# Wide weights for state times r, routing of four chunks at a time, other transfer splits and a re-planned order in a linear-attention and mixture-of-experts kernel

## The chip, the cores and the metric

One core of one Trainium2 chip runs the whole program in one launch. The metric is the device time in microseconds. The kernel before was run three times: 624.01 us median, 620.74 to 625.52.

## The reference

The first half is a recurrence over 768 time steps for 4 batches x 8 heads, head size 40, in float32. The second half routes each of the 3072 resulting rows of 320 values to one of 8 experts.

```python
for t in range(S):                                   # S = 768, state is [B,H,40,40]
    y[:, :, t] = einsum('bhd,bhde->bhe', r_t, state)
    Sa = einsum('bhde,bhe->bhd', state, a_t)
    state = state * w_t[:, :, None, :] - Sa (x) b_t + v_t (x) k_t
x = y as [3072, 320]
skip = x @ w_skip > 0 ; logits = x @ w_gate ; e = argmax(logits)
h = relu(x @ w1[e]) ; out = x + gate * (h @ w2[e])   # rows with skip > 0, else out = x
```

## The kernel before

**Tiling of the recurrence.** The 768 steps are cut into 24 chunks of 32 steps (`c`), two chunks to a block of 64 (`h`), four chunks to a phase (`ph`). The 32 batch-head pairs are two groups of 16 (`x` is 0 or 1, the upper and the lower partitions). Partitions 0 to 39 hold one half of the batches, 64 to 103 the other. Within a chunk the recurrence is solved in closed form: products of w by scans (`scan_z`, `scan_w`), small products of a, b and k (`m1`), the inverse of a triangular 32x32 system (`tinv`, on DVE), and then per chunk and group the chain that carries the state.

**The chain of one chunk.** `rs` multiplies the state by r (even chunks alone, for 64 steps), `ux` applies the left factors, `uq` the triangular inverse, followed by four ACT copies into the tile R1t and a POOL multiplication that masks R1t; `sst` makes the next state (ACT and DVE copies of it go to R1t and, in odd chunks, to the tile SS); `yy` makes the chunk's 128 x 320 output rows, which DVE scales into the tile XS and which SP writes to `out`. The two groups run half a chunk apart. `m2` multiplies v by r for the next chunk.

**SS and rs.** SS is [128, 2, 8, 40]: for each half of the batches a block whose other half of the partitions is zero. `rs` (line 534) runs 16 matmuls per group and even chunk, each with 40-column weights and 64 moving columns, alternating between output partitions 0 to 39 and 64 to 103.

**Routing.** After every second chunk `RP` (line 697) starts `route` (line 894) on two chunks: three transposes per chunk, `score` (line 869, 12 matmuls in four strips of 32 output partitions), `pick` (line 875, small DVE operations on 128 x 16 values), 8 matmuls that count rows per expert, more DVE operations, and one indirect POOL transfer per chunk that scatters the rows to the DRAM tensor `xg`. The last two chunks are routed one by one, in the gap between the two halves of the program.

**Transfers.** SP issues nearly all of them from one in-order queue: w, k and b, a (`load_w`, `load_kb`, `load_a`), v (`load_v`, line 366), zeros (`l1z`, line 405), the mask copies of `m1` (4 per call), the padding of `xg` (`pad`, line 860), expert weights (`load`, line 944), chunk outputs. The repeated copies of v and r (`load_rv`, line 357, `load_rr`, line 362) are issued by POOL except in the first chunk.

**What sets the order.** The recorder `Rec` (from line 62) collects all operations up to chunk 22, estimates each one's time with hand-fitted constants (line 68, `cost` at line 100, `pipe` at line 122 for transfers), and `plan` (line 184) lists them greedily by due time (`keys`, line 258). `flush` (line 262) then emits them in that order, so all planned operations carry line 272 in the profile; operations recorded outside the plan carry line 134. `plan` also has a model of the arrival of PE's instructions in blocks of 256 (constants BLK and SLOW).

**Experts.** From about 480 us on, each expert's weights are split into a high and a low part and two products per layer part are run on PE; rows are scattered to `out`.

Of the kernel before, what the change touches and what calls it, by code (L numbers as in the profile page):

```python
# [62 lines left out]
class Rec:  # L63
# [3 lines left out]
    HOP={'PA':0.066,'VA':0.034,'AV':0.033,'PV':0.11,'AP':0.053,'VP':0.055,'GP':0.054,'AG':0.08,'VG':0.13,'PG':0.17}  # L67
    EX=dict(V=0.08,P=0.07,A=0.0,G=0.0,S=0.0); PW=1.25; BLK=3.6; SLOW=0.8; BW=2.7e5; DSC=0.012; AHEAD=2.5
    def hop(s,e,f): return (0.114 if e=='V' else 0.0) if e==f else s.EX[e]+s.HOP.get(e+f,0.04)
# [30 lines left out]
    def cost(s,e,op,w,r,a):  # L100
        sz=lambda x: int(np.prod([d[1] for d in list(x.ap)[1:]])) if len(list(x.ap))>1 else 1
        n=max(sz(x) for x in (w[:1]+r[:1]))
        if 'dma' in op: return (1.06,2.6) if 'ind' in op else (0.63 if e=='S' else 0.55,2.2)
        ps=any('PSUM' in str(x.space).upper() for x in r)
        if e=='P':
            o=sz(w[0]); m=w[0].ap[0][1]
            if op=='transpose': return max(0.145,0.04+0.001*o),0
            if m<16: return 0.05+0.0016*o,0
            if m==16: return 0.022,0
            if m==32: return 0.034 if o<16 else 0.0098+0.00041*o,0  # L110
            if m<=48: return 0.0213+0.00072*o,0
            if m<=64: return max(0.072,0.028+0.00075*o),0
            return max(0.11,0.0021*o),0
        if e=='A': return 0.15+0.00085*n+(0.06+0.07*(n>99) if op=='activation' else 0.12 if abs(w[0].ap[-1][0])>8 and n>99 else 0.0),0
        if e=='G': return (0.08+n*0.0008 if op=='memset' else 0.18 if op=='tensor_copy' else 0.2+0.00195*n),0
        if op=='tensor_tensor_scan': return 0.02+0.00217*n,0
        if op=='transpose': return 0.08+0.00115*n*(1 if n<1000 else 1.6),0
        if op=='memset': return 0.04+0.0003*n,0
        if op=='reciprocal': return 0.17,0
        if op=='tensor_tensor': return (0.1 if ps and 'PSUM' not in str(w[0].space).upper() and n>199 else 0.06)+0.00105*n*(1 if ps or n<99 else 1.75),0  # L120
        return 0.12+0.00105*n,0
    def pipe(s,w,r):

        n=int(np.prod([d[1] for d in w.ap])); run=n
        for x in (w,r):
# [4 lines left out]
            run=min(run,q)  # L130
        p=w if 'DRAM' not in str(w.space).upper() else r
        return 4*n/min(6e5,5e3*max(16,p.ap[0][1]))+n/run*s.DSC/16
    def call(s,e,op,fn,a,k):
# [50 lines left out]
    def plan(s,keep=None):  # L184
# [33 lines left out]
        while done<N:  # L218
# [20 lines left out]
            if e=='P':  # L239
                pos+=t.k  # L240
                while pos>=256*(blk+1):
                    x=max(fin[i],ent+s.BLK); fin[i]=x; ent=x; blk+=1
            if t.L and e in 'VG': port[e]=fin[i]
# [3 lines left out]
            elif e=='G' and t.f==2: gi=-1.0  # L247
            if t.x: dq=max(dq,fin[i]+1.0)+t.x; lat=max(lat+t.x,dq+1.2-fin[i])
            for j in t.n:
# [6 lines left out]
        s.st,s.fin,s.bank_of,s.en,s.span=st,fin,bank,en,max(fin)  # L256
    LET=0.7; FAR=1.0; ALT=1.0; FILL=None
    def keys(s):
# [46 lines left out]
def attn(ctx,tc,i,m,out,X):  # L305
# [5 lines left out]
    pp=m.pp  # L311
# [26 lines left out]
    RW=(104,72)  # L338
    SS=[cp.tile([128,2,8,40],F32,name=f"SS{x}") for x in range(2)]
    eo=(0,64); ao=(64,0); uo=(96,32)  # L340
# [15 lines left out]
    rvt={}  # L356
    def load_rv(c,E=G):
        if c>=NC: return
        t=VV[0] if c%2==0 else RR[1] if c==1 else VV[1]
        rvt[c]=t.rearrange("p (u t) -> p u t",u=16); cutl(E,rvt[c],i['vv'][c],c<4,128)  # L360
    rrt={}
    def load_rr(h,E=G):

        if h>=NH: return
        rrt[h]=RR[h%2].rearrange("p (u t) -> p u t",u=16); cutl(E,rrt[h],i['rr'][h],h<2,128)
    def load_v(c,x):
        if c>=NC: return
        SP.dma_start(R1[x][c%NR1][ao[x]:ao[x]+32,:,0:40],i['vt'][c,x])
    def scan_z(h,dst=None,E=None,rv=rv):
# [35 lines left out]
    def l1z(h,x):  # L405
        if h>=NH: return
        SP.dma_start(L1[x][h%NL][ao[x]:ao[x]+32].rearrange('p u c t -> p (u c t)'),i['zer'][0:32,0:1024])
    def l1a(h,x,E=None):
# [125 lines left out]
    def rs(c,x):  # L534
# [5 lines left out]
        for hh in range(4):  # L540
            for b in (0,2,1,3):
                s=slice(64*(b//2),64*(b//2)+40); v=(b%2)*4+hh
                TE.matmul(RS[s,v,:],SS[x][:,b//2,v,:],rr[:,b%2,2*hh+x,:],start=True,stop=True)
        for bh in range(2):
# [26 lines left out]
    def sst(c,x):  # L571
# [22 lines left out]
        for bh in range(2):  # L594
            s=slice(64*bh,64*bh+40)
            A.copy(SS[x][s,bh],S2[s])
    Yt={}; XS={}
    def yy(c,x):
# [8 lines left out]
        if x==1:  # L607
            if cc==0: XS[c//2]=m.xp.tile([128,2,XW],F32,tag="XS",name="XS")
            xs=XS[c//2][:,cc,0:320]
            V.tensor_tensor(xs.rearrange("p (h e) -> p h e",h=8),Y,H[c//2]['WT',cc].rearrange("p h x e -> p (h x) e"),ALU.mult)  # L610
# [8 lines left out]
    if 1:  # L619

        with tc.manual_schedule(engines={ET.Pool}):
            rec.on=True
            z,zl=(SS[x].rearrange("p a b c -> p (a b c)") for x in range(2))
            fl=lambda t: t.rearrange("p u c t -> p (u c t)")
# [5 lines left out]
            V.memset(fk(KBa[0][96:128]),0.0); G.memset(fk(KBa[1][96:128]),0.0)  # L630
            V.memset(rv,0.0); V.memset(z[:,0:512],0.0); V.memset(zl,0.0)
            G.memset(WR[:,8192:10240],0.0)
# [6 lines left out]
            for x in range(2): load_v(0,x)  # L639
            load_rv(0,SP); load_rr(0,SP); load_kb(2)  # L640
            scan_z(0,None,V); scan_d(0); scan_w(0,V); load_w(2)
# [8 lines left out]
            for x in range(2): l1a(1,x,V)  # L650
            load_a(2,L1t[:,3072:4096].rearrange("p (u t) -> p u t",u=16)); load_rv(1,SP)
            for b in range(4): kbt(0,b)
# [6 lines left out]
            for x in range(2):  # L659
                for c in range(2): SP.dma_start(L2[x][0][64*x:64*x+64,c],i['idl'][x,64*x:64*x+64])  # L660
            load_kb(3); load_w(3,alt[:,0:1041]); load_a(3,a1)
# [7 lines left out]
            load_w(4); load_kb(4)  # L669
            G.memset(z[:,512:640],0.0); G.memset(L1t[:,2048:3072],0.0)  # L670
            m2(1,0); Tb(4); m2(1,1); Tb(3)
# [18 lines left out]
            for x in range(2):  # L690
                for c in range(2): SP.dma_start(L2[x][1][64*x:64*x+64,c],i['idl'][x,64*x:64*x+64])
        tg=iter(()); tn=[0]
# [4 lines left out]
        def RP(p):  # L697
            nonlocal rg
            if c%2==0 and c>0 and p==ROUTE[0]: rg=m.route(XS[c//2-1],2,c-2)
            if p in (RLAST[c-22] if c>21 else ROUTE[1+c%2]):  # L700
                if c>1 and p in RB[c%2]: burst(1,m.tri,m.mc[:,0:RN])
                next(rg,None)
        def last22():
            xl=XS[NC//2-1]
            def onehot(q): V.tensor_scalar(m.P[q],m.io,m.sl[:,0:1],None,ALU.is_equal)
            return xl,m.route(xl[:,0:1],1,NC-2,lambda: onehot(0)),onehot
        for c in range(NC):
# [93 lines left out]
            T()  # L801
            load_rv(c+2,G if c else SP)
            if c%2 or c==0: load_rr((c+3)//2,G if c else SP)
            if c<2: m.pad(2*c); m.pad(2*c+1)
# [42 lines left out]
class Moe:  # L847
# [12 lines left out]
    def pad(s,k):  # L860
        s.nc.sync.dma_start(s.xg.rearrange("(q p) d -> p q d",p=128)[:,4*k:4*k+4],s.i['xpad'].unsqueeze(1).broadcast_to([128,4,XW]))
    def xpose(s,X):
# [6 lines left out]
    def score(s,xT,sc):  # L869
        nc=s.nc  # L870
        lg=s.ps.tile([128,9],F32,tag="pp",name="lg")
        for k,(a,b) in enumerate(KT):
            for q in range(4): nc.tensor.matmul(lg[32*q:32*q+32],xT[:b-a,k,32*q:32*q+32],s.wg[:b-a,k,:],start=k==0,stop=k==2)
        nc.scalar.copy(sc,lg)
    def pick(s,pr,n,gate):
# [18 lines left out]
    def route(s,XS,n,c0,last=None):  # L894
# [246 lines left out]
```

## Time and profile before

| | us or share |
|---|---|
| median of 3 runs | 624.01 |
| the profiled execution's own time | 625.9 |
| its span, first to last instruction | 624.0 |
| PE busy | 470.0 (75%), 12424 matmuls |
| DVE busy | 472.7 (76%), 1269 |
| ACT busy | 390.0 (62%), 982 |
| POOL busy | 315.5 (51%), 285 |
| mean granted TensorE clock | 0.923 of full speed |
| DMA packets | 64360, 80.59 MB, 129 GB/s over the span |

PE is TensorE's matmul side, PEld its weight loads, DVE VectorE, ACT ScalarE, POOL GpSimd, SP SyncE. A busy PE is a modelled figure: matmuls overlap. Idle time is put down to the last releaser seen; "issue" means that the engine waited for nothing that the profile shows. Each float32 matmul of the program stands in the trace as two matmuls and two weight loads.

### The profile page before, as it was taken

To read this page: it belongs to the slowest core of one execution; us is meant where nothing else is said; L and a number is where in the kernel's file an instruction comes from. 1 tells how busy PE (TensorE), PEld (TensorE's weight loads), DVE (VectorE), ACT (ScalarE), POOL (GpSimd) and SP (SyncE) were. 2 spreads that over 40 slices of the span, in tenths; PEclk is the share of its full clock that TensorE was granted. 3 is DMA by queue.
4 is the path that set the end of the run, shared out by engine and by line. 5 is a ranking of instruction groups with operands and counts; after the bars stand their busy time and mean duration, and the time that the engine had idled before them with its cause. 6 is when DMAs were issued, how large, how long until landed. Compare 5 with 4: busy or idle time off the path is not lost. (4 is left out here: it accounts for less than half of the span.)

```text
span 624.0 us, 28751 instructions
## 1 busy us (share of the span) xinstructions
PE 470.0 (75%) x12424; PEld 407.5 (65%) x12424; DVE 472.7 (76%) x1269; ACT 390.0 (62%) x982; POOL 315.5 (51%) x285
## 2 busy tenths in 40 slices
PE   0154327877787887887887789878977999999992
PEld 0143216666666666776776677667765799999992
DVE  6525894789997987998989879865783558898860
ACT  7073216878695877887696769577865455555510
POOL 4133626437491868477583853234223266666751
PEclk9997757899897998998798989989988999999997
DMA  8997232433452453425351534453663477775100
GB/s 190 251 270 226 78 99 65 130 81 92 93 137 75 108 143 100 133 67 147 87 153 40 144 98 109 101 153 95 167 168 93 123 220 232 240 225 156 43 18 18
DMA packets 64360, 80.59 MB, mean 129 GB/s; under 512 B 33698, under 2 KB 52719, under 8 KB 63124
## 3 DMA queue, kind: packets, MB, share of 16 engines
q1 hardware_dynamic: 58323, 64.55, 38.6%
q0 software_dynamic: 5904, 14.15, 8.2%
q8 instruction: 99, 1.62, 1.2%
q14 instruction: 34, 0.27, 0.1%
HBM read 67.80 MB, written 13.15 MB: 130 GB/s over the span
## 5 line engine op out<-in xcount | busy, mean ns | idle before, releaser
L272 ACT COPY R1t<-pc 32x288 f32<-32x288 f32 (+4 forms) x254 | 98.8, 389 | 38.1 <-PE pc L272 32.4
L272 POOL TENSOR_TENSOR R1t<-R1t,mc 64x512 f32<-64x512 f32 x43 | 55.5, 1292 | 70.9 <-ACT R1t L272 64.7
L272 DVE TENSOR_TENSOR px<-px,M 128x168 f32<-128x168 f32 (+10 forms) x240 | 61.2, 265 | 2.3
L134 POOL TENSOR_TENSOR WL<-WR,WH 128x1280 fp32r<-128x1280 f32 (+1 forms) x21 | 57.8, 2794 | 8.6 <-ACT WH L134 8.6
L272 POOL TENSOR_TENSOR WR<-WR,M 104x1024 f32<-104x1024 f32 x19 | 41.6, 2207 | 35.5 <-DVE M L272 22.9
L272 DVE TENSOR_TENSOR M<-M,px 128x168 f32<-128x168 f32 (+10 forms) x240 | 54.4, 255 | 2.0 <-DVE px L272 0.2
L272 DVE TENSOR_TENSOR_SCAN M<-M 104x1041 f32<-104x1041 f32 (+1 forms) x20 | 47.0, 2348 | 0.2
L272 ACT COPY R1t<-pq 32x256 f32<-32x256 f32 (+4 forms) x101 | 36.2, 358 | 8.4 <-PE pq L272 5.3
L134 ACT CAST WH<-WR 128x1024 fp32r<-128x1024 f32 (+1 forms) x35 | 39.6, 1132 | 0.0
L272 POOL DMA_INDIRECT xg<-XS,ix x20 | 24.1, 1206 | 29.9 <-DMA xg<-XS,ix 11.7
L134 POOL DMA_INDIRECT out<-ro,ti x16 | 15.8, 989 | 44.3 <-DVE ro L134 10.7
L272 PE MATMUL pc<-UX,TB 32*32 32x104 f32 (+1 forms) x1024 | 30.2, 245 | 9.0 <-issue 7.9
L134 ACT ACTIVATE hH<-pc 128x512 fp32r<-128x512 f32 x21 | 12.6, 599 | 37.8 <-PE pc L134 37.8
L134 DVE CAST ti<-xe 128x2 int32<-128x2 f32 x8 | 35.0, 4376 | 0.2
L272 PE MATMUL py<-L2t,R1t 128*32 128x40 f32 x1344 | 23.4, 208 | 12.1 <-issue 9.4
L134 PE MATMUL pc<-xH,WH 128*128 128x256 f32 x126 | 32.5, 283 | 0.0
L272 DVE TENSOR_TENSOR R1t<-pc,D 40x512 f32<-40x512 f32 (+1 forms) x44 | 26.6, 605 | 6.3 <-PE pc L272 4.2
L134 DVE TENSOR_TENSOR WL<-WR,WH 128x1024 fp32r<-128x1024 f32 (+1 forms) x19 | 23.8, 1253 | 9.9 <-ACT WH L134 9.4
L272 ACT COPY R1t<-ps 40x288 f32<-40x288 f32 (+4 forms) x72 | 27.5, 383 | 5.4 <-PE ps L272 4.2
L272 PE MATMUL ps<-R1t,L2t 128*40 128x72 f32 (+1 forms) x672 | 28.6, 233 | 2.8 <-ACT R1t L272 1.6
L272 PEld LDWEIGHTS pc<-UX,TB 32*32 32x32 f32 x1024 | 21.5, 107 | 14.0 <-issue 10.1
L272 PEld LDWEIGHTS py<-L2t,R1t 128*32 128x32 f32 x1344 | 17.7, 114 | 16.3 <-issue 11.7
(353 smaller groups left out, 1537.0 us busy)
## 6 DMA issues: line engine op xcount, KB each, us to landing
WR<-w SPq DMA_DIRECT2D x16, 640.0 KB
WR<-w SPq DMA_DIRECT2D x16, 512.0 KB
WR<-kb SPq DMA_DIRECT2D x16, 320.0 KB
WR<-w SPq DMA_DIRECT2D x16, 256.0 KB
R1t<-vt SPq DMA_DIRECT2D x48, 80.0 KB
out<-XS SPq DMA_DIRECT2D x24, 160.0 KB
rrt<-rr POOLq DMA_DIRECT2D x20, 160.0 KB, 5.4
vvt<-vv POOLq DMA_DIRECT2D x20, 160.0 KB, 6.1
```

What stands on the lines that cost most here:

```text
L134: if not s.on: return fn(*a,**k)
L272: for fn,a,k,own in s.tasks[i].calls: (fn if s.en[i]==s.tasks[i].e else s.nc.vector.tensor_copy)(*[at(x,own) for x in a],**{n:at(x,own) fo ...
```

## The change

The state tile becomes [128, 8, 104]: both halves of the batches stand on the diagonal of one 104-column block, and `rs` runs 8 matmuls with 104-column weights where it ran 16 with 40. Routing takes four chunks at a time (chunks 0 to 19), then two, then one and one; score and counting use the full 128 output partitions in place of four strips. `load_rv` and `load_rr` move from POOL's queue to SP's. The DRAM side of several transfers (v, zeros, the identity blocks, padding, the weights of experts 0 and 1) gets an outer dimension of 8. The planner's constants and its transfer model change, and with them the order of everything up to chunk 22. The scratch that software-issued transfers get is set to 4096 bytes a partition.

```diff
-    EX=dict(V=0.08,P=0.07,A=0.0,G=0.0,S=0.0); PW=1.25; BLK=3.6; SLOW=0.8; BW=2.7e5; DSC=0.012; AHEAD=2.5
+    EX=dict(V=0.08,P=0.07,A=0.0,G=0.0,S=0.0); PW=1.25; BLK=3.4; SLOW=0.0; BW=2.0e5; AHEAD=2.5; LAND=1.7
...
-        if 'dma' in op: return (1.06,2.6) if 'ind' in op else (0.63 if e=='S' else 0.55,2.2)
+        if 'dma' in op: return (1.06,2.6) if 'ind' in op else (0.63 if e=='S' else 0.55,0.0)
...
-        p=w if 'DRAM' not in str(w.space).upper() else r
-        return 4*n/min(6e5,5e3*max(16,p.ap[0][1]))+n/run*s.DSC/16
+        return max(4*n/s.BW,n/run*0.002)
...
-                    x=max(fin[i],ent+s.BLK); fin[i]=x; ent=x; blk+=1
+                    x=max(fin[i],ent+s.BLK+s.SLOW*min(8.0,max(0.0,dq-ent))); fin[i]=x; ent=x; blk+=1
...
-            if t.x: dq=max(dq,fin[i]+1.0)+t.x; lat=max(lat+t.x,dq+1.2-fin[i])
+            if t.x:
+                a=fin[i]+(0.5 if e=='S' else 1.5); b=max(dq,a); dq=b+t.x
+                if t.x<0.3: b=a+0.4*(b-a)
+                lat=b+t.x+s.LAND-fin[i]
...
-    LET=0.7; FAR=1.0; ALT=1.0; FILL=None
+    LET=0.7; FAR=1.25; ALT=1.0; FILL=None
...
-    SS=[cp.tile([128,2,8,40],F32,name=f"SS{x}") for x in range(2)]
+    SS=[cp.tile([128,8,104],F32,name=f"SS{x}") for x in range(2)]
...
-    def load_rv(c,E=G):
+    def load_rv(c,E=SP):
...
-    def load_rr(h,E=G):
+    def load_rr(h,E=SP):
...
-        SP.dma_start(R1[x][c%NR1][ao[x]:ao[x]+32,:,0:40],i['vt'][c,x])
+        SP.dma_start(R1[x][c%NR1][ao[x]:ao[x]+32,:,0:40],i['vt'][c,x].rearrange('(a b) u d -> a b u d',a=8))
...
         for hh in range(4):
-            for b in (0,2,1,3):
-                s=slice(64*(b//2),64*(b//2)+40); v=(b%2)*4+hh
-                TE.matmul(RS[s,v,:],SS[x][:,b//2,v,:],rr[:,b%2,2*hh+x,:],start=True,stop=True)
+            for b in range(2): TE.matmul(RS[0:104,b*4+hh,:],SS[x][:,b*4+hh,:],rr[:,b,2*hh+x,:],start=True,stop=True)
...
-            A.copy(SS[x][s,bh],S2[s])
+            A.copy(SS[x][s,:,64*bh:64*bh+40],S2[s])
...
-            if cc==0: XS[c//2]=m.xp.tile([128,2,XW],F32,tag="XS",name="XS")
-            xs=XS[c//2][:,cc,0:320]
+            if c%4==0: XS[c//4]=m.xp.tile([128,4,XW],F32,tag="XS",name="XS")
+            xs=XS[c//4][:,c%4,0:320]
...
-            if c%2==0 and c>0 and p==ROUTE[0]: rg=m.route(XS[c//2-1],2,c-2)
+            if c%4==0 and c>0 and p==ROUTE[0]: rg=m.route(XS[c//4-1],4,c-4)
+            if c==22 and p==ROUTE[0]: rg=m.route(XS[5][:,0:2],2,20)
...
                 next(rg,None)
+                if c<22: next(rg,None)
...
-            load_rv(c+2,G if c else SP)
-            if c%2 or c==0: load_rr((c+3)//2,G if c else SP)
+            load_rv(c+2)
+            if c%2 or c==0: load_rr((c+3)//2)
...
-        s.nc.sync.dma_start(s.xg.rearrange("(q p) d -> p q d",p=128)[:,4*k:4*k+4],s.i['xpad'].unsqueeze(1).broadcast_to([128,4,XW]))
+        s.nc.sync.dma_start(s.xg.rearrange("(q p) d -> p q d",p=128)[:,4*k:4*k+4],s.i['xpad'].rearrange('(a b) d -> a b d',a=8).unsqueeze(2).broadcast_to([8,16,4,XW]))
...
-            for q in range(4): nc.tensor.matmul(lg[32*q:32*q+32],xT[:b-a,k,32*q:32*q+32],s.wg[:b-a,k,:],start=k==0,stop=k==2)
+            nc.tensor.matmul(lg,xT[:b-a,k,:],s.wg[:b-a,k,:],start=k==0,stop=k==2)
...
-        rk=s.ps.tile([128,2*n,8],F32,tag="pp",name="rk")
-        for q in range(4): nc.tensor.matmul(rk[32*q:32*q+32,0:n,:],s.tri[:,32*q:32*q+32],oh,start=True,stop=True)
-        for q in range(4): nc.tensor.matmul(rk[32*q:32*q+32,n:2*n,:],s.one[:,0:32],oh,start=True,stop=True)
+        rk=s.ps.tile([128,n+1,8],F32,tag="pp",name="rk")
+        nc.tensor.matmul(rk,s.tri,s.oh[:,0:n+1],start=True,stop=False)
+        for j in range(n): nc.tensor.matmul(rk[:,j+1:n+1],s.one,oh[:,j].unsqueeze(1).broadcast_to([128,n-j,8]),start=False,stop=j==n-1)
         ps=wk.tile([128,n,8],F32,tag="pos",name="pos")
-        for j in range(n):
-            nb=wk.tile([128,8],F32,tag="base",name="base",bufs=3)
-            V.tensor_tensor(ps[:,j],rk[:,j],s.base,ALU.add)
-            V.tensor_tensor(nb,rk[:,n+j],s.base,ALU.add); s.base=nb
+        V.tensor_tensor(ps,rk[:,0:n],s.base.unsqueeze(1).broadcast_to([128,n,8]),ALU.add)
+        nb=wk.tile([128,8],F32,tag="base",name="base",bufs=3)
+        V.tensor_tensor(nb,rk[:,n],s.base,ALU.add); s.base=nb
...
+        n=8 if e<2 else 16
+        for k in range(2): SP.dma_start(r[:,1024*k:1024*k+1024],s.i['w1'][e,128*k:128*k+128].rearrange('(a b) f -> a b f',a=n))
...
-    nc = bacc.Bacc("TRN2", target_bir_lowering=False, num_devices=1)
+    nc = bacc.Bacc("TRN2", target_bir_lowering=False, num_devices=1, dynamic_dma_scratch_size=4096)
```

## Rows read from the trace of the kernel before

**Rows 1.** Stretches: length, then busy us (count) of PE, PEld, DVE, ACT, POOL; clock, DMA.
```profile
0.00:60.00 60.00, 15.57 (x364) 13.35 (x364) 29.81 (x34) 29.96 (x70) 19.20 (x18) 0.95 0.90 240
60.00:100.00 40.00, 14.60 (x630) 12.31 (x631) 32.85 (x62) 9.81 (x29) 18.30 (x27) 0.59 0.29 82
100.00:480.00 380.00, 308.74 (x10402) 255.13 (x10399) 312.93 (x1036) 288.34 (x797) 202.38 (x202) 0.94 0.44 113
480.00:624.00 144.00, 131.07 (x1040) 126.71 (x1033) 97.14 (x138) 61.87 (x87) 75.59 (x39) 0.97 0.47 139
...
400.00:480.00 80.00, 65.19 (x2139) 53.02 (x2137) 52.77 (x159) 58.13 (x163) 24.99 (x25) 0.94 0.49 134
140.00:400.00 260.00, 210.85 (x6995) 174.95 (x6996) 230.16 (x783) 197.50 (x546) 159.82 (x161) 0.93 0.43 109
```

**Rows 2.** Waits from 100 to 480 us: waiter, releaser, us in total, times, longest.
```profile
PEld pc L272 <- issue: 17.9, 32, 3.9
PEld py L272 <- issue: 11.7, 15, 3.3
PEld pq L272 <- issue: 6.7, 16, 1.6
PEld ps L272 <- issue: 5.9, 20, 1.3
...
POOL R1t L272 <- ACT R1t L272: 64.7, 17, 11.4
```

**Rows 3.** Page, DMA queues: packets, MB, share of 16 engines.
```profile
q8 instruction: 99, 1.62, 1.2%
```

**Rows 4.** Timeline from 184 to 200 us: start, us, work, idle before it and releaser.
```profile
196.54 1.19 PE L272 MATMUL pc<-UX,TB 32*32 32x104 f32 x31 [3.78 <-issue]
197.66 1.08 PE L272 MATMUL pc<-WR,L1t 128*32 128x64 f32 x32
197.78 2.02 ACT L272 COPY R1t<-pc 32x416 f32<-32x416 f32 x4 [5.14 <-PE pc L272]
...
199.88 1.28 POOL L272 TENSOR_TENSOR R1t<-R1t,mc 64x512 f32<-64x512 f32 x1 [11.37 <-ACT R1t L272]
```

**Rows 5.** Whole span, instructions on SS, then on xT, then on oh alone.
```profile
0.00:624.00 624.00, 26.60 (x704) 22.91 (x704) 2.53 (x5) 17.25 (x41) 0.20 (x1) 0.92 0.48 129
...
0.00:624.00 624.00, 12.27 (x576) 9.69 (x576) 3.90 (x12) 10.04 (x36) 0.92 0.48 129
...
0.00:624.00 624.00, 4.43 (x208) 3.31 (x208) 10.88 (x39) 0.92 0.48 129
```

**Rows 6.** PE timeline of single groups: start, us, work.
```profile
226.79 0.22 PE L272 MATMUL pq<-rrt,SCR 128*64 128x32 f32 x1
...
125.64 0.66 PE L272 MATMUL pc<-rrt,SCR 128*64 128x32 f32 x16
...
115.93 0.69 PE L272 MATMUL pc<-rrt,vvt 128*64 128x64 f32 x16
...
117.84 1.09 PE L272 MATMUL pq<-rrt,SS 128*40 128x64 f32 x32 [0.28 <-ACT R1t L272]
...
139.03 0.49 PE L272 MATMUL pq<-wg,xT 128*32 128x9 f32 x24
...
263.58 0.32 PE L272 MATMUL ps<-oh,mc 128*32 128x16 f32 x16
```

**Rows 7.** DVE timeline of a routing of two chunks: start, us, work.
```profile
159.60 0.18 DVE L272 TENSOR_TENSOR eq<-sc,mx 128x16 f32<-128x16 f32 x1
159.70 0.17 DVE L272 TENSOR_TENSOR sb<-sc,mx 128x16 f32<-128x16 f32 x1
```

**Rows 8.** POOL groups from 100 to 480 us: busy, mean ns, idle before and releasers.
```profile
L272 POOL DMA_INDIRECT xg<-XS,ix x20 | 24.1, 1206 | 29.9 <-DMA xg<-XS,ix 11.7 <-DVE px L272 7.8 <-PE pc L134 4.9
...
L272 POOL DMA_DIRECT2D vvt<-vv x20 | 11.0, 557 | 7.2 <-PE pc L272 6.2 <-PE pq L272 1.0
L272 POOL DMA_DIRECT2D SCR<-vv x20 | 10.8, 548 | 14.3 <-PE pc L272 9.1 <-PE pq L272 4.6 <-PE ps L272 0.6
L272 POOL DMA_DIRECT2D rrt<-rr x18 | 9.2, 518 | 0.0
```

**Rows 9.** Timeline of SP's queue from 60 to 300 us.
```profile
102.62 0.60 SPq L272 DMA_DIRECT2D R1t<-vt  x1
```

**Rows 10.** DMA issues up to 60 us: work, count, KB each.
```profile
xg<-xpad SPq DMA_DIRECT2D x3, 644.0 KB
```

More of the change, by code (lines that the diff above doesn't have):

```diff
@@ L406, in l1z @@
         if h>=NH: return
-        SP.dma_start(L1[x][h%NL][ao[x]:ao[x]+32].rearrange('p u c t -> p (u c t)'),i['zer'][0:32,0:1024])
+        SP.dma_start(L1[x][h%NL][ao[x]:ao[x]+32].rearrange('p u c t -> p (u c t)'),i['zer'][0:32,0:1024].rearrange('(a b) f -> a b f',a=8))
     def l1a(h,x,E=None):
@@ L622, in attn @@
             rec.on=True
-            z,zl=(SS[x].rearrange("p a b c -> p (a b c)") for x in range(2))
+            z,zl=(SS[x].rearrange("p a b -> p (a b)") for x in range(2))
             fl=lambda t: t.rearrange("p u c t -> p (u c t)")
@@ L630, in attn @@
             V.memset(fk(KBa[0][96:128]),0.0); G.memset(fk(KBa[1][96:128]),0.0)
-            V.memset(rv,0.0); V.memset(z[:,0:512],0.0); V.memset(zl,0.0)
+            V.memset(rv,0.0); V.memset(z,0.0); V.memset(zl,0.0)
             G.memset(WR[:,8192:10240],0.0)
@@ L639, in attn @@
             for x in range(2): load_v(0,x)
-            load_rv(0,SP); load_rr(0,SP); load_kb(2)
+            load_rv(0); load_rr(0); load_kb(2)
             scan_z(0,None,V); scan_d(0); scan_w(0,V); load_w(2)
@@ L650, in attn @@
             for x in range(2): l1a(1,x,V)
-            load_a(2,L1t[:,3072:4096].rearrange("p (u t) -> p u t",u=16)); load_rv(1,SP)
+            load_a(2,L1t[:,3072:4096].rearrange("p (u t) -> p u t",u=16)); load_rv(1)
             for b in range(4): kbt(0,b)
@@ L659, in attn @@
             for x in range(2):
-                for c in range(2): SP.dma_start(L2[x][0][64*x:64*x+64,c],i['idl'][x,64*x:64*x+64])
+                for c in range(2): SP.dma_start(L2[x][0][64*x:64*x+64,c],i['idl'][x,64*x:64*x+64].rearrange('(a b) u d -> a b u d',a=8))
             load_kb(3); load_w(3,alt[:,0:1041]); load_a(3,a1)
@@ L669, in attn @@
             load_w(4); load_kb(4)
-            G.memset(z[:,512:640],0.0); G.memset(L1t[:,2048:3072],0.0)
+            G.memset(L1t[:,2048:3072],0.0)
             m2(1,0); Tb(4); m2(1,1); Tb(3)
@@ L690, in attn @@
             for x in range(2):
-                for c in range(2): SP.dma_start(L2[x][1][64*x:64*x+64,c],i['idl'][x,64*x:64*x+64])
+                for c in range(2): SP.dma_start(L2[x][1][64*x:64*x+64,c],i['idl'][x,64*x:64*x+64].rearrange('(a b) u d -> a b u d',a=8))
         tg=iter(()); tn=[0]
@@ L702, in RP @@
                 next(rg,None)
+                if c<22: next(rg,None)
         def last22():
-            xl=XS[NC//2-1]
+            xl=XS[5][:,2:4]
             def onehot(q): V.tensor_scalar(m.P[q],m.io,m.sl[:,0:1],None,ALU.is_equal)
@@ L886, in pick @@
         m2=wk.tile([128,n],F32,tag="m2",name="m2"); V.reduce_max(m2,eq,axis=AX.X)
-        oh=wk.tile([128,n,8],F32,tag="oh",name="oh"); V.tensor_tensor(oh,eq,b3(m2),ALU.is_equal)
+        oh=wk.tile([128,5,8],F32,tag="oh",name="oh"); V.memset(oh[:,n],0.0); s.oh=oh; oh=oh[:,0:n]; V.tensor_tensor(oh,eq,b3(m2),ALU.is_equal)
         V.scalar_tensor_tensor(oh,pr[:,:,8:9].broadcast_to([128,n,8]),0.0,oh,ALU.is_gt,ALU.mult)
@@ L946, in load @@
         SP=s.nc.sync; r=s.raw[e%2]
-        for k in range(2): SP.dma_start(r[:,1024*k:1024*k+1024],s.i['w1'][e,128*k:128*k+128])
-        for k in range(2): SP.dma_start(r[64*k:64*k+64,2048:3072],s.i['w1'][e,256:320])
-        for k in range(2): SP.dma_start(r[:,3072+1280*k:4352+1280*k].rearrange("p (k d) -> p k d",k=4),s.i['w2'][e,512*k:512*k+512].rearrange("(k p) d -> p k d",p=128))
+        n=8 if e<2 else 16
+        for k in range(2): SP.dma_start(r[:,1024*k:1024*k+1024],s.i['w1'][e,128*k:128*k+128].rearrange('(a b) f -> a b f',a=n))
+        for k in range(2): SP.dma_start(r[64*k:64*k+64,2048:3072],s.i['w1'][e,256:320].rearrange('(a b) f -> a b f',a=n))
+        for k in range(2): SP.dma_start(r[:,3072+1280*k:4352+1280*k].rearrange("p (k d) -> p k d",k=4),s.i['w2'][e,512*k:512*k+512].rearrange("(k a b) d -> a b k d",k=4,a=n))
     def base_last(s):
```

## The prediction

> **What bounds the kernel now.** First the busy times by stretch [rows 1]. Four stages show. Up to 60 us the transfers are the full resource (share 0.90, 240 GB/s). From 60 to 100 us it is DVE (32.9 of 40). From 100 to 480 us no engine is full: PE 308.7, DVE 312.9, ACT 288.3 and POOL 202.4 of 380. From 480 us PE is busy 131 of 144, and the change touches next to nothing there. So the change is decided between 100 and 480 us. Which engine sets that stage's pace can be read from its two parts: from 140 to 400 us DVE is busy 89% of the time, after 400 us only 66%, yet PE stays at 81% in both and runs 26.9 and 26.7 matmuls per us. Emptying DVE by a quarter did not speed PE up. I therefore count PE's time nearly in full, DVE's and POOL's at about a quarter.
>
> Then the waits of this stage [rows 2]. What stops PE's weight loads most often is "issue": 17.9 + 11.7 + 6.7 + 5.9 = 42.2 us in 83 stalls. The page has 99 instruction packets on one queue [rows 3], and PE runs 2 x 12424 = 24848 weight loads and matmuls, about 251 a packet. Between 100 and 480 us that makes 2 x 10402 / 251 = 83 packets: as many as stalls. I read them as PE waiting for its next packet, 0.51 us each. The timeline shows what a long one does [rows 4]: PE stops inside `uq` for 3.78 us, ACT then stands 5.14 us and POOL 11.37 us.
>
> **The change, part by part.** The sum is made against the profiled execution's 625.9 us (span 624.0); the median, 624.01, is 1.9 lower.
>
> *Fewer PE instructions.* SS is read by 704 recorded matmuls: 22 groups (11 even chunks, two x) of 32, two records per matmul of the code [rows 5]. They become 352. The 576 score records (24 per chunk) become 144, the 208 counting records 64 (five routings of four chunks at 10, one of two at 6, two of one at 4). That is 928 matmuls and as many weight loads, 1856 of 24848 instructions, 7.4 packets. At 0.51 us a stall they give 3.8 us. Two more effects lower the stalls that stay. PE work that grows (next part) by 20 us over 76 packets can fill up to 0.26 us of each stall; I take half, 10 us. And a packet's transfer shares its engine with data for 0.44 of the time [rows 1]; if data moves to fewer engines and the packets' engine is not among them, up to 0.44 of the remaining 28 us goes. No view shows engine numbers, so I take half of that, 6 us. Together -20; ends 0 (nothing on the path) and -42 (all stalls).
>
> *Wider PE weights.* The trace has no 104-wide weights with few moving columns. Nearest are the groups of v times r: 16 passes in two halves side by side, 8 steps with 64-wide weights; they take 0.66 us with 32 moving columns and 0.69 with 64 [rows 6]. The moving columns hardly count, so the weights set the step: with the last pass at 0.22 us, (0.66 - 0.22)/7 = 0.063 us, 1 ns a column. Then 104 columns cost 0.10 us and 128 cost 0.126. `rs` now takes 1.09 us for 32 passes, two side by side; after, 16 passes one after the other, 15 x 0.10 + 0.22 = 1.72: +0.63, times 22 = +14. Score: 5 x 0.126 + 0.22 = 0.85 against 0.49, times 24 = +8.6. Counting: 1.35 against two times 0.32 in five routings, 0.85 against 0.32 in one, 0.60 against 0.32 in two, +4.7. Upper end +27. Lower end -1: if moving columns set the step as in today's `rs` ((1.09 - 0.22)/15 = 0.058 us), `rs` stays at 1.09 us and score and counting keep their strips' pace. I take +20: the 64-wide row is the nearest, less a quarter, because a group's first weights can load while the group before runs.
>
> The Trainium skill speaks against the change here: "TensorE: Matmul & The Clock Gate", section "LDWEIGHTS (loading the stationary operand)", gives the load as columns divided by 1.2 in ns, whatever the rows, so 87 ns for 104 columns and 107 for 128; the 64-wide row agrees (53 ns against 63). By it the three would add 9.6 + 6.4 + 3.6 = +20 in place of +27, less a quarter +15 in place of +20.
>
> *DVE.* A routing of two chunks runs 18 small operations, one of four 17; ten of the first kind become five of the second, 95 fewer. They start 0.10 us apart and last 0.17 to 0.18 [rows 7], so 9.5 to 17 us of DVE. At a quarter: -3; ends 0 and -17.
>
> *POOL.* The 58 plain transfers issued there from 100 to 480 us cost 11.0 + 10.8 + 9.2 = 31.0 us of busy time and held POOL 7.2 + 14.3 = 21.5 us for buffers that PE was still reading [rows 8]. Queued behind them are the R1t masks, for which `yy` and `sst` wait. But in 17 of some 46 masks POOL was ready and waited for ACT, 64.7 us in all [rows 2]; only the others can have been late. -8; ends 0 and -21.5.
>
> *SP.* It gets these 58 issues at 0.60 us [rows 9], +35 us, and their waits for buffers, with `m1`'s mask copies and v queued behind. SP is otherwise idle or waiting, so this costs only where a needed copy is next: +2; ends 0 and +10 (half of the 21.5).
>
> *Scatters.* Of 20 scatters half follow another directly; now three in four do, 5 more, each behind the one before for 11.7/6 = 1.95 us [rows 8]: 10 us of POOL, with masks behind. +2; ends 0 and +10.
>
> *Start.* Up to 60 us 240 GB/s x 60 = 14.4 MB move [rows 1], of which padding is 1.9 MB [rows 10] and identity and v by the code some 1.0 MB. If those 2.9 MB go to 8 engines, the busiest get (14.4 - 2.9)/16 + 2.9/8 = 1.08 MB in place of 0.90, 20% more, up to +12 us. But padding is needed only by the first scatter and most of it was issued late, and DVE sets the next 40 us. 0; ends -5 and +12. State zeroing, the larger XS and the smaller scratch cost nothing here: the first lies under the loads of the start, the others are space; without that cover the zeroing is under 1 us.
>
> *New order.* No row prices it. One stall as in [rows 4] either way is some 10 us; the plan now has a landing time of its own, so -3; ends -10 and +10.
>
> *Expert stage.* PE sets it; the weights of experts 0 and 1 arrive on fewer engines but are asked for well before 480 us: 0; ends 0 and +6.
>
> Sum: -20 + 20 - 3 - 8 + 2 + 2 + 0 - 3 = -10: 615.9 profiled, **614** as a median.
>
> **The rivals.** (1) The instruction supply sets the whole pace: 7.4 packets at 380/83 = 4.6 us each, -34, the wider weights hidden under it and the rest -10: 580, up to 600 if half so. For it: a stall for each packet. Against: PE is busy 81%. (2) No change: wider weights eat what the supply gives, and the chain PE, ACT, POOL of `uq` keeps its pace because neither POOL nor DVE decided it: 620 to 626. For it: the 64.7 us that POOL waits for ACT. (3) Slower: the array becomes the bound. The 104- and 128-wide weights cost their full +27, and only the 3.8 us come back, with -3 - 8 + 4 from the others: +16, 640. For it: the flat 0.66 and 0.69; it decides if an `rs` group takes 1.7 us and the issue waits stay over 35 us. (4) Slower through transfers: fewer engines for the loads, +12 at the start and +8 behind SP's head: 634. For it: the 0.90 share up to 60 us. The split could also do nothing, if the number of engines doesn't follow that dimension; then the 6 us of the supply go and so does this rival: 620.
>
> The Trainium skill has a rule on this: "DMA: Bandwidth & Descriptors", section "Why a DMA increments its semaphore by 16 and not by 1", says that the engines used are the largest number up to 16 that divides both sides' slowest dimensions, and on SP's queue the lowest-numbered ones. By that rule the split does what it says; no row here shows it.
>
> **How the numbers follow.** Two runs of one kernel differ by under 1%, so 1% is what can be told. Forecast: 0.50 (0.44 of it under 617.8), own range 605 to 620. Rival 1: 0.12, faster. Rival 2, with the split that does nothing: 0.20, within 1%. Rivals 3 and 4: 0.09 each, slower. Faster 0.56, within 1% 0.26, slower 0.18. The range from 596 to 633 leaves out most of rival 1 and of rival 3 and the far side of 4, some 0.2.
>
> **What would show it.** In the trace after: 11496 matmuls and some 92 instruction packets; `rs` groups of 16 at about 1.7 us (right) or 1.1 (wrong); PEld's issue waits from 42 to about 22 us; POOL without plain transfers after the start; DVE less by 10 to 17 us. The prediction is wrong if the issue waits hardly fall, if the first chunk's output comes later than before, or if the stage's length follows DVE or POOL.

## The result and the profile after

The changed kernel takes **607.22 us** (median of four runs, 602.21 to 612.9) beside 624.21 for the kernel before: a ratio of 0.971, 95% interval 0.963 to 0.979. In two later groups of runs it gave 0.970 (0.961 to 0.978) and 0.973 (0.968 to 0.978). Forecast were 614, a range of 596 to 633 and a narrower one of 605 to 620. Some executions take over 1.5% longer than the fastest of their kernel, many of them at a lower granted clock; the ratios, and the medians in the first column of the table of experiments, leave them out.

The profiled execution took 606.73 us, with a span of 604.7. By stretch (columns as in [rows 1]):

```profile
0.00:60.00 60.00, 19.66 (x552) 16.76 (x552) 56.76 (x77) 36.02 (x87) 33.94 (x34) 0.87 0.75 206
60.00:100.00 40.00, 24.42 (x1005) 21.13 (x1005) 25.94 (x69) 20.22 (x56) 15.81 (x15) 0.69 0.60 165
100.00:462.00 362.00, 314.00 (x8923) 267.67 (x8924) 284.72 (x884) 272.62 (x755) 166.31 (x137) 0.94 0.42 114
462.00:604.00 142.00, 134.73 (x1024) 129.22 (x1023) 99.63 (x141) 61.85 (x87) 75.38 (x39) 0.97 0.47 141
```

The change was expected to be decided in the third stretch. The largest difference stands in the first: DVE is busy 56.8 of 60 us where it was busy 29.8 [rows 1]. Where the time went is read best from the one instruction that writes each chunk's output. These are the VectorE groups of it, the first two lines of before and the last two of after: count, shortest, median and longest in ns, then the start of the first and the last in us. The first line of each pair holds chunks 0 to 20, the second 21 to 23:

```profile
L272 DVE TENSOR_TENSOR XS<-py,WT x21: 475/491/494, 111.9 to 444.3; 128x320 f32<-128x320 f32 x21
L134 DVE TENSOR_TENSOR XS<-py,WT x3: 491/492/493, 461.9 to 480.2; 128x320 f32<-128x320 f32 x3
```

```profile
L274 DVE TENSOR_TENSOR XS<-py,WT x21: 473/485/493, 96.2 to 415.9; 128x320 f32<-128x320 f32 x21
L133 DVE TENSOR_TENSOR XS<-py,WT x3: 492/492/492, 443.4 to 462.8; 128x320 f32<-128x320 f32 x3
```

| stretch | before | after | difference |
|---|---|---|---|
| start, to the first output | 111.9 | 96.2 | -15.7 |
| first to 21st output | 332.4 | 319.7 | -12.7 |
| 21st to 22nd output | 17.6 | 27.5 | +9.9 |
| 22nd to 24th output | 18.3 | 19.4 | +1.1 |
| last output to the end | 143.8 | 141.9 | -1.9 |

So the 19.3 us of the two spans are three things: a shorter start, a faster middle, and 10 us given back in one place.

**The start.** Waits of DVE up to 60 us, before (waiter, releaser, us in total, times, longest):

```profile
DVE M L272 <- ACT M L272: 17.3, 3, 11.0
DVE XS L272 <- DMA mc<-mc: 10.7, 1, 10.7
```

After, none of them is over 0.8 us. In the timeline of DVE (start, us, work, idle before it and releaser; two lines of before, then two of after), the transposes that before began at 46.49 us, behind an 11 us wait, begin at 29, and the copy from `mc` that before stopped DVE for 10.7 us until 22.4 stands at 40:

```profile
22.40 0.25 DVE L272 COPY XS<-mc 128x2 f32<-128x2 f32 x2 [10.68 <-DMA mc<-mc]
...
46.49 0.32 DVE L272 STREAM_TRANSPOSE M<-pc 128x128 f32<-128x128 f32 x1 [10.99 <-ACT M L272]
```

```profile
28.99 0.29 DVE L274 STREAM_TRANSPOSE M<-pq 128x128 f32<-128x128 f32 x1
...
40.16 2.07 DVE L274 COPY XS<-mc 128x4 f32<-128x4 f32 x1
```

The 11 us wait for ScalarE goes back to transfers as well. In PE's queue before (timeline: start, us, work, idle before it and releaser) the products of v and r stand ahead of the work that DVE is waiting for, and PE waits for their loads:

```profile
30.26 1.12 PE L272 MATMUL pc<-rrt,vvt 128*64 128x64 f32 x16 [6.83 <-DMA rrt<-rr]
...
39.66 1.07 PE L272 MATMUL pq<-rrt,rrt 128*64 128x32 f32 x16 [6.54 <-DMA rrt<-vv]
```

An early instruction that waited for a late transfer held everything behind it on its engine. After, these products begin at 35.93 and 46.19 us, behind the work that they held up. On SP's queue the first loads of v and r for them are issued at 21.50 and 21.90 us (before at 7.94 and 12.44), the next ones (`R1t<-vt`) from 37.24 (14.79) and the identity blocks from 40.88 (27.48), while the third load of w comes at 12.38 in place of 21.86. The transfers spread out, 0.75 and 0.60 of the DMA engines' time in the first two stretches where [rows 1] has 0.90 and 0.29.

**The 10 us given back.** POOL from 412 us, then PE's weight loads (timeline: start, us, work, idle before it and releaser):

```profile
412.65 1.01 POOL L274 DMA_INDIRECT xg<-XS,ix  x1 [0.16 <-issue]
...
418.47 0.98 POOL L274 DMA_INDIRECT xg<-XS,ix  x1 [4.81 <-DMA xg<-XS,ix]
...
426.67 0.97 POOL L274 DMA_INDIRECT xg<-XS,ix  x1 [7.22 <-DMA xg<-XS,ix]
429.43 1.26 POOL L274 TENSOR_TENSOR R1t<-R1t,mc 64x512 f32<-64x512 f32 x1 [1.79 <-DMA xg<-XS,ix]
430.74 0.60 PEld L133 LDWEIGHTS py<-L2t,R1t 128*32 128x32 f32 x32 [8.60 <-POOL R1t L274]
```

The scatters of chunks 16 to 19 stand in a row (the first of them is at 407.41, with one mask behind it). The third and the fourth wait until the one before has landed. The next R1t mask is queued behind them, and `yy` on PE waits 8.6 us for the mask. The wait also costs clock: the granted clock is 1.00 from 400 to 420 us, 0.81 from 420 to 430, where PE is busy 1.5 us, and 0.50, its lower level of 1.2 GHz, from 430 to 435.

**PE.** Three groups in the timeline after, which answer to [rows 6]: score, `rs`, counting for four chunks:

```profile
399.27 0.93 PE L274 MATMUL pc<-wg,xT 128*128 128x9 f32 x6
...
400.13 1.68 PE L274 MATMUL pq<-rrt,SS 128*104 128x64 f32 x16
...
403.76 1.28 PE L274 MATMUL pq<-oh,mc 128*128 128x40 f32 x10
```

Instructions on SS, on xT and on oh over the whole span, which answer to [rows 5]:

```profile
0.00:604.70 604.70, 38.26 (x352) 35.30 (x352) 4.92 (x9) 15.55 (x37) 0.92 0.48 133
...
0.00:604.70 604.70, 22.21 (x144) 20.08 (x144) 3.77 (x10) 10.12 (x38) 0.92 0.48 133
...
0.00:604.70 604.70, 9.12 (x64) 8.43 (x64) 6.51 (x32) 0.92 0.48 133
```

And the weight loads' instruction waits from 100 to 462 us, with the page's row of packets ([rows 2, 3] before):

```profile
PEld pc L274 <- issue: 12.0, 26, 1.8
...
PEld pq L274 <- issue: 5.2, 14, 1.1
PEld ps L274 <- issue: 4.7, 16, 0.9
PEld py L274 <- issue: 2.4, 9, 0.6
```

```profile
q8 instruction: 92, 1.51, 1.1%
```

Most of this is as forecast: 16 passes in 1.68 us (1.72), 92 packets, 11496 matmuls, waits of 24.3 us in place of 42.2 (22). A score takes 0.93 us (0.85). The three wider groups cost PE 11.7 + 9.9 + 4.7 = 26.3 us more in the records, where the sum had 20.

### The profile page after: what moved, and what is told of

It reads as the page before. It is cut to its first block, busy times and chain, and to the rows that moved or that the text cites. A ratio compares the mean times of both kernels' runs of the same rounds, so it can differ in the third digit from the quotient of the medians.

```text
span 604.7 us, 26781 instructions
## 1 busy us (share of the span) xinstructions
PE 492.8 (81%) x11496; PEld 434.8 (72%) x11496; DVE 467.0 (77%) x1168; ACT 390.7 (65%) x984; POOL 291.4 (48%) x223
## 5 line engine op out<-in xcount | busy, mean ns | idle before, releaser
L274 ACT COPY R1t<-pc 32x416 f32<-32x416 f32 (+4 forms) x235 | 91.2, 388 | 26.9 <-PE pc L274 17.3
L274 ACT COPY R1t<-pq 32x256 f32<-32x256 f32 (+4 forms) x119 | 46.6, 392 | 9.0 <-PE pq L274 7.0
L274 POOL DMA_INDIRECT xg<-XS,ix x20 | 22.0, 1101 | 41.7 <-DMA xg<-XS,ix 29.1
L133 POOL DMA_INDIRECT out<-ro,ti x16 | 15.7, 984 | 45.7 <-PE py L133 13.2
L133 DVE CAST ti<-xe 128x2 int32<-128x2 f32 x8 | 37.3, 4658 | 0.2
L274 PE MATMUL pc<-UX,TB 32*32 32x104 f32 (+1 forms) x896 | 25.3, 250 | 5.2 <-issue 3.5
L274 PE MATMUL pc<-rrt,SS 128*104 128x64 f32 x240 | 26.6, 266 | 2.3 <-DVE base L274 1.7
L274 PE MATMUL ps<-R1t,L2t 128*40 128x40 f32 (+1 forms) x672 | 26.2, 227 | 2.0 <-issue 1.6
L133 PE MATMUL ps<-WH,hH 128*128 128x320 f32 x88 | 27.5, 313 | 0.0
L274 POOL TENSOR_TENSOR M<-M,mc 128x256 f32<-128x256 f32 x20 | 19.9, 1000 | 15.0 <-issue 6.0
L133 PE MATMUL ps<-WL,hH 128*128 128x320 f32 x88 | 27.1, 308 | 0.0
```

Source lines behind the costliest of these rows:

```text
L133: if not s.on: return fn(*a,**k)
L274: for fn,a,k,own in s.tasks[i].calls: (fn if s.en[i]==s.tasks[i].e else s.nc.vector.tensor_copy)(*[at(x,own) for x in a],**{n:at(x,own) fo ...
```

## The experiments

Theory A: the gain is the new order of the start, and the operations matter little. Theory B: it is the operations (fewer PE instructions, POOL relieved, fewer engines per transfer). Three groups of runs, each on one chip with its own runs of the kernel before:

| run | us (executions counted) | median of all | before beside it | ratio, 95% |
|---|---|---|---|---|
| order alone | 608.2 (7 of 10) | 609.9 | 614.5 | 0.990, 0.985 to 0.995 |
| operations alone | 617.8 (1 of 4) | 628.6 | 614.5 | none |
| splits undone | 604.4 (5 of 10) | 606.6 | 614.5 | 0.984, 0.978 to 0.990 |
| narrow `rs` and score | 601.1 (4 of 4) | 601.1 | 614.5 | 0.978, 0.968 to 0.989 |
| after again | 605.8 (4 of 4) | 605.8 | 623.6 | 0.970, 0.961 to 0.978 |
| POOL issues the loads | 614.4 (3 of 4) | 614.7 | 623.6 | 0.981, 0.971 to 0.991 |
| masks before scatters | 601.1 (4 of 5) | 602.3 | 623.6 | 0.960, 0.950 to 0.969 |
| the same, and narrow | 597.9 (4 of 4) | 597.9 | 623.6 | 0.956, 0.945 to 0.967 |
| after, third | 604.6 (5 of 6) | 604.9 | 622.6 | 0.973, 0.968 to 0.978 |
| splits undone again | 601.8 (2 of 6) | 611.6 | 622.6 | 0.975, 0.966 to 0.984 |
| order again | 610.2 (5 of 6) | 612.0 | 622.6 | 0.982, 0.976 to 0.988 |
| routing of two | 597.1 (3 of 6) | 600.2 | 622.6 | 0.956, 0.948 to 0.964 |

**The order alone, twice.** Before's operations with after's whole `Rec` class.

```diff
-BLK=3.6; SLOW=0.8; BW=2.7e5; DSC=0.012; AHEAD=2.5
+BLK=3.4; SLOW=0.0; BW=2.0e5; AHEAD=2.5; LAND=1.7
-    LET=0.7; FAR=1.0; ALT=1.0; FILL=None
+    LET=0.7; FAR=1.25; ALT=1.0; FILL=None
 ... (and cost, pipe and the transfers in plan, as in the change)
```

> The operations of before, put in order by the planner's costs and transfer model of after; PE's first 53 groups then stand in the same order as after's. Theory A (the gain is the new order of the start): the first chunk's output leaves VectorE at 95 to 99 us in place of 111.9, and the time is 607 to 613. Theory B (the gain comes from the operations: fewer PE instructions, POOL relieved of transfers, transfers on fewer engines): first output 108 to 113, time 620 to 628.

> The order alone, beside after. Theory A (start from the order, the rest from the operations): first output at 95 to 99 us, then before's pace; 8 to 15 us faster than before and 4 to 9 us slower than after. Theory B' (the order alone is all of the gain): within 3 us of after.

The outputs of the second one:

```profile
L274 DVE TENSOR_TENSOR XS<-py,WT x21: 473/483/493, 96.6 to 433.1; 128x320 f32<-128x320 f32 x21
L133 DVE TENSOR_TENSOR XS<-py,WT x3: 491/492/493, 451.0 to 470.2; 128x320 f32<-128x320 f32 x3
```

First output at 96.6 us (97.9 in the first), then 336.5 us to the 21st, before's pace; 17.9 to the 22nd. It gains 6.3 us in one group and 12.4 in the other, and after is 5.6 below it. The start is the order's work, and it is worth less in time than the 14 to 15 us by which the first output comes earlier.

**The operations alone.** After with before's `Rec` class (the reverse of that diff).

> The operations and transfers of after, put in order by the planner's costs of before. Theory A: the first output stays at 108 to 113 us and the time at 618 to 626, since the later stage gains 2 us at most. Theory B: 605 to 612, with PE's instruction waits from 100 to 460 us near 22 us as in after. If both the order and the operations are needed together, both this kernel and the order alone stay above 617.

```profile
L272 DVE TENSOR_TENSOR XS<-py,WT x21: 470/483/492, 113.4 to 438.7; 128x320 f32<-128x320 f32 x21
L134 DVE TENSOR_TENSOR XS<-py,WT x3: 491/491/492, 464.7 to 485.8; 128x320 f32<-128x320 f32 x3
```

The first output is late again, 113.4 us. The middle, 325.3 us, is below before's 332.4 at a mean granted clock of 0.891 (before 0.923), but the step from the 21st to the 22nd output is 26.0 us (before 17.6). Its time stays open: the one execution that counts took 617.78 us, no less than before's 614.5. In the traces the answer agrees with the order alone: the order makes the start, the operations the middle and the loss behind it. That the operations alone gain any time is not shown; the 2 us that theory A left them for the later stage are fewer than the 7 us of the middle.

**The splits undone, twice.** Identity, v, zeros, padding and expert weights as in before; the order of work on all five engines stays after's.

```diff
-...i['vt'][c,x].rearrange('(a b) u d -> a b u d',a=8))
+...i['vt'][c,x])
 ... (idl, zer, xpad, w1 and w2 likewise)
```

> After with every split of a transfer undone (identity, v, zeros, padding, expert weights written as in before); all five engines issue the same work in the same order as in after. If the split matters as the prediction had it (6 us of instruction supply, nothing at the start): 610 to 616 and the weight loads' instruction waits from 22 to 26 to 34 us. If the split is what brings the first output forward: first output over 100 us, time over 612. If it does nothing: 603 to 610, first output 95 to 98 us.

> The splits undone once more, now beside after. If fewer engines for some transfers free the instruction packets (the prediction's 6 us) this kernel is 4 to 8 us slower than after, and the weight loads' instruction waits from 100 to 460 us are 26 us or more. If the splits do nothing: within 3 us of after and waits of 20 to 25 us.

Instruction waits in the second one, 100 to 460 us:

```profile
PEld pc L274 <- issue: 10.5, 27, 1.5
...
PEld ps L274 <- issue: 6.5, 17, 1.2
...
PEld pq L274 <- issue: 3.7, 14, 0.8
...
PEld py L274 <- issue: 1.3, 6, 0.3
```

22.0 us in these four beside 24.3 in after; the first time it was 26.2, at the edge of the band for an effect. The two intervals of the third group cover each other, but there the kernel's 601.8 us rest on two executions of six, and the median of all six, 611.6, is above after's 604.9. So the waits show no gain from the splits, and the times leave a loss or a gain of 1% open. How many engines a transfer used was not seen.

**Narrow `rs` and score.** The planner is given the wide version's numbers, so the order is after's on every engine.

```diff
-            for b in range(2): TE.matmul(RS[0:104,b*4+hh,:],SS[x][:,b*4+hh,:],...)
+            for b in (0,2,1,3):
+                s=slice(64*(b//2),64*(b//2)+40); v=(b%2)*4+hh
+                TE.matmul(RS[s,v,:],SS[x][:,v,s],rr[:,b%2,2*hh+x,:],...)
-            nc.tensor.matmul(lg,xT[:b-a,k,:],...)
+            for q in range(4): nc.tensor.matmul(lg[32*q:32*q+32],xT[:b-a,k,32*q:32*q+32],...)
```

> After with the state times r as 32 matmuls of 40-wide weights, two side by side, and the score as four strips of 32, in the same order on all engines. Array time falls by 22 x 0.58 + 24 x 0.44 = 23 us and 784 matmul records and their weight loads come back, 6.2 instruction packets. If PE's array sets the pace: 585 to 597. If instruction supply sets it (4.4 us of PE per packet): 620 to 635. If PE is off the path between these groups, or the two cancel as the prediction's terms have it (-17 of array, +3 to +12 of supply): 593 to 609, with the instruction waits back above 30 us.

Its instruction waits from 100 to 460 us:

```profile
PEld pc L274 <- issue: 11.7, 30, 1.4
PEld pq L274 <- issue: 11.6, 15, 2.4
...
PEld ps L274 <- issue: 5.4, 16, 1.7
PEld py L274 <- issue: 2.9, 8, 0.7
```

It runs 784 more matmul records and 98 packets. PE is busy 13.2 us less on SS and 9.5 less on xT; the waits grow from 24.3 to 31.6 us. The time is 3.3 us below the kernel with the splits undone beside it, which differs from it in the splits too: in the forecast's band, though the waits passed 30 only just. The intervals of the two overlap (0.968 to 0.989 and 0.978 to 0.990). A second pair, below, gives 3.2 us of the same sign, its intervals overlapping too. So the change's wide state and score weights look like a net loss of some 3 us, and are at best no gain that could be seen.

**POOL issues the loads.** v and r from POOL again, planned as in after.

```diff
-            load_rv(c+2)
+            load_rv(c+2,SG if c else SP)     # SG: planned as SP, issued on POOL; load_rr likewise
```

> The changed kernel itself, so that the variants stand beside it on one chip. Every theory: 601 to 609, first output at 95 to 99 us, 288 to 294 us from the first to the 19th output and 54 to 59 us from the 19th to the 22nd.

> After with the 50 or so loads of v and r issued by POOL again, at their places in the same order of work; PE, VectorE and ScalarE run the same instructions in the same order. If POOL's relief is worth the 8 us of the prediction: 610 to 618, and the stretch from the first to the 19th output grows from 291 to 296 to 303 us. If POOL waits for ScalarE anyway and the relief is worth nothing: 602 to 609 and that stretch within 4 us of after.

The waits for buffers are back on POOL (100 to 460 us):

```profile
POOL SCR L274 <- PE pc L274: 12.1, 3, 6.3
POOL vvt L274 <- PE pc L274: 8.3, 3, 6.0
```

614.4 beside 605.8 for after: 8.6 us (609.1 to 615.0 in the executions that count, after 604.9 to 607.3). This is POOL's relief and SP's added work together, forecast as -8 and +2: real, and somewhat larger than forecast. The trace has a mean granted clock of 0.888 (after 0.92), so its stretches are not compared. After again has 97.5 us to the first output, 290.6 from there to the 19th and 56.2 to the 22nd, as every theory said.

**Masks before scatters, and with narrow.** The last two scatters planned are held back until two masks have been issued; PE, VectorE, ScalarE and SP keep their order.

```diff
+        skip=[i for _,i in sorted(work) if s.tasks[i].f==1][-2:]; s.late=[x for i in skip for x in s.tasks[i].calls]
+            if i in skip: continue
-            uq(c-1,1); T()
+            uq(c-1,1); T(); c==22 and [fn(*a,**k) for fn,a,k,own in rec.late]...
```

> After with one thing moved: the third and fourth scatter of chunks 16 to 19 go behind two R1t masks on POOL; the other engines keep their instructions and order. If the four scatters in a row are what holds PE for 8.4 us before chunk 20's last output group (POOL waits 4.8 and 7.2 us for the scatter before): the gap between the 21st and 22nd output falls from 27.4 to 18 to 22 us and the time by 5 to 9, to 595 to 602. If something else holds that place (the weights of expert 0 on their way, VectorE's splits): the gap stays over 25 us and the time within 3 us of after.

> The moved scatters and the narrow state times r and score together, a version meant to beat both kernels. If the two gains are independent: 590 to 597 (about 6 for each). If both shorten the same chain and do not add: 596 to 602.

POOL in the second of them, and its outputs:

```profile
416.58 1.28 POOL L274 TENSOR_TENSOR R1t<-R1t,mc 64x512 f32<-64x512 f32 x1 [2.75 <-DVE XS L274]
423.46 1.33 POOL L133 TENSOR_TENSOR R1t<-R1t,mc 64x512 f32<-64x512 f32 x1 [5.61 <-PE pc L133]
424.95 1.27 POOL L727 DMA_INDIRECT xg<-XS,ix  x1 [0.16 <-POOL R1t L133]
429.48 0.97 POOL L727 DMA_INDIRECT xg<-XS,ix  x1 [3.25 <-DMA xg<-XS,ix]
```

```profile
L274 DVE TENSOR_TENSOR XS<-py,WT x21: 474/486/493, 98.4 to 416.0; 128x320 f32<-128x320 f32 x21
L133 DVE TENSOR_TENSOR XS<-py,WT x3: 485/491/493, 435.7 to 454.2; 128x320 f32<-128x320 f32 x3
```

These two masks no longer wait behind scatters, and the gap falls from 27.5 to 19.7 us (19.0 in the trace of the first, at a granted clock of 0.64). The first takes 601.1 us where after takes 605.8: 4.7 us, just short of the 5 to 9 forecast. Narrow groups on top give 597.9, another 3.2. That lies in the band named for gains that do not add; but narrow groups alone gave 3.3, so it is rather each gain that is smaller than the 6 us taken for it, and the noise cannot tell the two. This version beats both kernels: none of its executions is over 601.6 us.

**Routing of two.** After with chunks routed in pairs.

```diff
-            if c%4==0 and c>0 and p==ROUTE[0]: rg=m.route(XS[c//4-1],4,c-4)
-            if c==22 and p==ROUTE[0]: rg=m.route(XS[5][:,0:2],2,20)
+            if c%2==0 and c>0 and p==ROUTE[0]: rg=m.route(XS[(c-2)//4][:,(c-2)%4:(c-2)%4+2],2,c-2)
-                if c<22: next(rg,None)
```

> The changed kernel again, as the one that the three other kernels of this group are measured against on one chip. Every theory: a ratio of 0.965 to 0.98 to the kernel before.

> After with one part undone: chunks are routed two at a time, as before; wide state, score and counting weights, transfers on SP and the planner's model stay. VectorE gets some 95 small operations back (10 to 17 us of its busy time), POOL never has more than two scatters of one routing in a row. If scatters in a row cost what the traces suggest (10 us before the 22nd output): the stretch from the 19th to the 22nd output falls from 56 to 45 to 50 us, and the time is 3 to 9 us below after. If the small operations matter more: the stretch from the first to the 19th output grows from 291 to 297 or more and the time is 2 to 8 us above after. If both hold, they cancel within 3 us and the two stretches show it.

```profile
L274 DVE TENSOR_TENSOR XS<-py,WT x21: 474/484/493, 96.5 to 413.8; 128x320 f32<-128x320 f32 x21
L133 DVE TENSOR_TENSOR XS<-py,WT x3: 493/493/493, 431.7 to 453.3; 128x320 f32<-128x320 f32 x3
```

The gap falls to 17.9 us, the 19th to 22nd output from 56.3 (after, third) to 44.6, and the first to 19th stays at 290.6 (289.3 and 290.7 in after), although VectorE works 249.3 us from 100 to 386 us where after works 239.5. POOL waits for scatters nearly as long as in after, 25.7 us in 9 waits from 100 to 460 us beside 29.1 in 11, the longest 4.9; but no mask that PE needs stands behind the long ones, and the longest wait of PE's weight loads for POOL's mask from 386 to 460 us is 0.6 us where it was 8.6.

597.1 beside 604.6, with intervals that do not meet (600.2 beside 604.9 over all executions). The list was planned anew here, so the order of all engines differs from after's: taking four chunks at a time, with the order that the planner makes of it, costs 4.7 to 7.5 us, and no gain from its saved VectorE work is seen. Routing of two together with narrow groups was not run.

## Why the prediction was near, and where it was wrong

The direction held, and the time roughly (607.2 for 614; profiled 606.73 for 615.9). The sum was near partly because misses of both signs met.

| term | predicted | measured |
|---|---|---|
| start and new order | 0 and -3 | -6.3 and -12.4 in time with the order alone; its first output at 96.6 and 97.9 in place of 111.9 |
| fewer PE instructions and wider weights, net | 0 | +3.3 and +3.2 for `rs` and score, each within the noise |
| DVE routing | -3 | no gain seen, with the order planned anew |
| POOL and SP | -8 and +2 | -8.6 together |
| transfers on fewer engines (in the first term) | -6 | not seen |
| scatters in a row | +2, up to +10 | +9.9 in the trace, 4.7 to 7.5 in time |
| expert stage | 0 | -1.9 |

**New order: the failed step.** "No row prices it" was wrong: rows of the same trace show what a new order could free, though not how much of it the order would reach. DVE stood 10.7 and 17.3 us in the first 60 us for one transfer and for ScalarE's late work, which itself waited for PE and PE for the loads of v and r; the prediction saw only that transfers were the full resource there. A stretch with a full DMA share can still be shortened if transfers are in the wrong order. Of the start it asked what fewer engines would add, never what waited. It took -3 with ends of -10 and +10; the order alone gave -6.3 and -12.4, with a start 14 to 15 us shorter and a middle no faster than before's.

**PE's time "nearly in full": failed.** The wide groups cost what was forecast, even in full, with no quarter hidden (+26.3 against an upper end of 27), yet undoing two of them gave back 22.7 us of PE and some 3 us of time. Even net of the 7.3 us of instruction waits that come back, about a fifth counts. The test on which it rested, PE at 81% both with a full and with an emptier DVE [rows 1], showed that DVE is not the bound; it did not show that PE is. Rival 2 had a part of this: the runs fit its view that the chain PE, ACT, POOL of `uq` sets the pace (in after, POOL's masks still wait 51.7 us for ScalarE from 100 to 400 us), but no run changes that chain by itself, so this is argued and not shown. Rival 2 was wrong that POOL decides nothing: what relieves POOL's queue counts fully. What relieves VectorE shows no gain.

The Trainium skill, "TensorE: Matmul & The Clock Gate", section "LDWEIGHTS (loading the stationary operand)", gives columns divided by 1.2 in ns: 87 ns for 104 columns, 107 for 128. The groups here take (1.68 - 0.22)/15 = 97 ns for 104 columns and (1.28 - 0.22)/9 = 118 ns for 128 in counting, between that rule and the prediction's 1 ns a column, and (0.93 - 0.22)/5 = 142 ns for 128 in score, above both.

**The instruction waits** fell as forecast, 42.2 to 24.3, but not for the reason given to 6 us of it: with the splits undone they are 26.2 and 22.0, and with narrow groups they return in part (31.6). The operations lower them and not the order: with the order alone they stay at 18.3 + 11.8 + 10.4 + 4.0 = 44.5 us, and with the operations alone they are 18.8. I read this as longer array work hiding the wait for the next packet, which gains little, since the time is then in the array; no run shows it by itself, and with routing of two, whose array work is much the same, they are 16.4. Rival 1, 580 us, falls with it. Rival 3 needed waits over 35 us, and rival 4 a later start; neither came.

**Scatters: mis-sized.** 1.95 us for each that follows another was the mean, and it held: 17.1 us in 9 waits from 100 to 400 us, the longest 4.4. From 412 to 430 us, where loads of expert weights of up to 512 KB are on their way, it was 4.8 and 7.2 us, and there the mask behind them is on PE's path. That the loads make the scatters slow is not shown. The term's upper end was the price, and the question "who waits behind it, and when" had been asked only of the mean.

**Open.** After is 5.6 us below the order alone. POOL's relief (-8.6), routing of four (+7.5) and the wide groups (+3.3) make +2.2; so some 8 us of gain are not assigned; they may lie in the counting, in the transfers' other queue position or in how the list falls out with the new operations. A change of any operation also shifts the planned list, except in the runs whose order was held (splits, narrow, POOL's loads, masks).

## What to carry to other kernels

Before a stage is written off as bound by transfers, list what its engines wait for: an instruction placed early for a late load blocks all behind it on its queue, and reordering loads and first uses gave the largest shortening of a stage here. Ask of every group of transfers that waits for its own predecessor which instruction stands behind it in the queue and what it holds up, at the busiest place and not on the mean. An engine that is 81 to 87% busy need not set the pace: undo some of its work with the order held and see what comes back.

## What the runs showed of the hardware

Consecutive indirect scatters into one DRAM tensor, each of which waits for the one before, cost POOL 1.9 us a wait in the middle of after (longest 4.4), 2.9 with routing of two (longest 4.9), and 4.8 and 7.2 us at one place while weight loads of 512 KB ran (DMA share 0.64 from 412 to 430 us, 0.48 in the 32 us before). Float32 matmuls with 104 weight columns and 64 moving columns step at 97 ns; with 128 they step at 118 ns in counting (up to 40 moving columns) and 142 ns in score (9 moving columns). After a stretch of 10 us with PE busy 1.5 us, the granted clock was 0.50, the lower of its two levels (1.2 GHz), for the next 5 us; before that stretch it had been 1.00. The loads of v and r issued by SP instead of POOL were worth 8.6 us with the order of PE, VectorE and ScalarE held.
